# Softmax over tokens on phi as it is loaded, with a maximum from slice comparisons, and filler matmuls tied to other events

## The chip, the cores and the metric

The kernel runs on one core of one Trainium2 chip. The metric is the device time of one execution in microseconds (us), and the median of three runs is quoted. The engines are TensorE (PE in the profile, its weight loads PEld), VectorE (DVE), ScalarE (ACT), GpSimd (POOL) and SyncE (SP), which here only issues transfers.

## The reference, cut to what matters

```python
a = phi - np.max(phi, axis=2, keepdims=True)      # phi [4, 8, 576, 32]: over the 576 tokens
a = np.exp(a)
a = a / (np.sum(a, axis=2, keepdims=True) + 1e-09)
k_m = np.einsum('bhsm,bhsd->bhmd', a, k)          # 32 memory rows for each head
v_m = np.einsum('bhsm,bhsd->bhmd', a, v)
scores = scale * np.matmul(q, k_m.transpose(0, 1, 3, 2))
...                                               # softmax over the 32, times v_m
x = (x @ w_a) * (x @ w_b) @ w_out                 # first gated layer, 2304 x 512, d_ff 1536
...                                               # second one: h * sigmoid(1.702 h), d_ff 2048
```

## The kernel before

**Units.** The attention is worked off in eight units, one for each batch and half of the heads: unit n is batch n // 2, heads 4 (n % 2) to 4 (n % 2) + 3. A tile of phi for a unit holds 128 partitions of tokens (`[P, HG, C0, M]`, 4 heads by 5 chunks of tokens by 32 columns); odd partitions have 4 chunks, and the fifth of theirs is filled once at the start. `memory(n)` takes a unit from phi to the 32 rows of keys and values of each head (`bdk`, `bdv`) and on to the scores; `queries(n)` transposes q for it; `softmax` makes the attention weights and marks them `attn`.

**memory(n) before.** phi is turned so that tokens lie along the free dimension: in units 0 and 1 by 20 matmuls against the identity (L552), in units 2 to 7 by a copy (L540 on GpSimd or L542 on ScalarE) and five transposes (L549). VectorE reduces the maximum over 512 and 64 tokens from PSUM (L556, L558) and joins them (L560). ScalarE takes the exponential with the sum beside it (L562, L566). Five more transposes turn it back (L570, L574), two copies bring it from PSUM into phi's tile (recorded in the helper `copy`, L330 and L332), and 20 matmuls multiply it with keys and values (L590). The result is scaled (L604 or L606), transposed (L612), copied, and multiplied with the queries (L629).

**The first gated layer.** Weights arrive as 64-bit words in pieces (`raw`) and are decoded by two ScalarE instructions and one of VectorE (L438, L442, L444). `fold(g, b)` multiplies the weights of column group g with `bdv` of batch b (L792), `fold_out` splits the product (L810, L812) and `gated` multiplies it with the attention weights (L844). A group needs four decoded pieces, a fold the `bdv` of two units. The rest of the layer and the second one follow (L1006, L1281, L1482, L1513).

**What sets the order.** No engine is scheduled at run time. While the program is built, a planner (`Order`) runs all of these as streams with priorities. It has a clock for each engine and a cost for each step, and emits at each turn the step that it thinks can start first. Loads have modelled landings: `load` adds size / rate to a running DMA time (first value `od.dma`, in ns) and then a latency, both from `RATE0` in this stage. Each engine then executes its instructions in the order that was emitted, and waits for data at run time. The order of the loads is the list `FIRST`: phi, keys and values, and q of units 0 and 1, then raw pieces 0 to 5, then unit 2, and so on.

**Fillers.** The stream `warm_up` has the lowest priority and puts matmuls of the identity with itself into TensorE's order: 18 at once (L1578), then, from the mark `phi 0` (the modelled landing of phi) until the weights of group 0 are decoded, wherever the planner sees TensorE free, each with a planned cost of 300 ns (L1582). Each of these matmuls is two instructions in the profile.

## Time and profile before

| | |
|---|---|
| median of three runs | 744.67 us (744.63 to 747.3) |
| the profiled execution | 744.51 us; span from first to last instruction 742.7 us, so 1.8 us lie around it |
| TensorE | 732.1 us busy (99%), chain that ended last 92% TensorE |
| VectorE, ScalarE, GpSimd | 533.2, 430.8, 386.1 us busy |
| granted TensorE clock | 0.999 in the mean |

Matmuls of fillers count as busy, so TensorE's share of the first 30 us says nothing about useful work. In a row of the profile a number after x is a count of instructions; a bracket at the end of a timeline row is the idle time of that engine ahead of the row and what ended it.

### The profile page before, as it was taken

To read this page: it belongs to the slowest core of one execution; us is meant where nothing else is said; L and a number is where in the kernel's file an instruction comes from. 1 tells how busy PE (TensorE), PEld (TensorE's weight loads), DVE (VectorE), ACT (ScalarE), POOL (GpSimd) and SP (SyncE) were. 2 spreads that over 40 slices of the span, in tenths; PEclk is the share of its full clock that TensorE was granted. 3 is DMA by queue.
4 is the path that set the end of the run, shared out by engine and by line. 5 is a ranking of instruction groups with operands and counts; after the bars stand their busy time and mean duration, and the time that the engine had idled before them with its cause. 6 is when DMAs were issued, how large, how long until landed. Compare 5 with 4: busy or idle time off the path is not lost.

```text
span 742.7 us, 14507 instructions
## 1 busy us (share of the span) xinstructions
PE 732.1 (99%) x5344; PEld 682.7 (92%) x5344; DVE 533.2 (72%) x799; ACT 430.8 (58%) x842; POOL 386.1 (52%) x347
## 2 busy tenths in 40 slices
PE   9899999999999999999999999999999999999997
PEld 8787888888889999999999999999998888999997
DVE  2987777568983447945898666666665697898884
ACT  3678664667863456546866655565656654544441
POOL 0324366447996616914998621333240296776660
PEclk9999999999999999999999999999999999999999
DMA  8998954786778966676525575544699954544411
GB/s 276 343 327 254 322 190 160 224 280 231 256 237 264 313 195 170 171 211 191 186 100 163 180 227 162 163 136 150 210 377 301 328 157 138 189 143 143 143 26 33
DMA packets 110359, 153.53 MB, mean 207 GB/s; under 512 B 8400, under 2 KB 89040, under 8 KB 110288
## 3 DMA queue, kind: packets, MB, share of 16 engines
q1 hardware_dynamic: 104928, 143.13, 60.3%
q10 hardware_dynamic: 5360, 9.47, 3.9%
q8 instruction: 42, 0.69, 0.4%
q14 instruction: 29, 0.24, 0.1%
HBM read 100.01 MB, written 52.56 MB: 205 GB/s over the span
## 4 chain that ended last, share of the span: by engine, by line
PE 92%; DMA 3%; POOL 2%; DVE 2%; SPq 1%; issue 0%; ACT 0%; DVEq 0%; POOLq 0%
PE bank L1281 24%; PE bank L844 21%; PE bank L1006 16%; PE bank L1513 14%; PE bank L1482 12%; PE bank L792 3%; DMA q<-in_q_dram 1%; PE bank L590 1%; DMA raw_p<-in_moe_w_b_dram 1%; DMA kv<-in_k_dram 1%; PE bank L509 1%; POOL w L339 1%; SPq L372 1%; POOL attn L339 1%; DVE attn L339 0%
## 5 line engine op out<-in xcount | busy, mean ns | idle before, releaser
L844 PEld LDWEIGHTS bank<-attn,eff 128*128 128x128 f32 x1152 | 154.3, 188 | 16.2 <-issue 6.1
L844 PE MATMUL bank<-attn,eff 128*128 128x288 f32 x1152 | 163.1, 298 | 0.5 <-DVE eff L812 0.5
L339 POOL TENSOR_TENSOR acc<-acc 128x512 f32<-128x512 f32 (+2 forms) x65 | 95.0, 1481 | 68.2 <-DVE w L339 27.9
L1323 DVE TENSOR_TENSOR acc<-bank,acc 128x384 f32<-128x384 f32 x168 | 89.8, 553 | 46.3 <-PE bank L1281 40.8
L339 DVE TENSOR_TENSOR w<-acc,w 128x512 fp32r<-128x512 f32 (+2 forms) x100 | 105.0, 1076 | 20.5 <-ACT w L345 20.4
L345 ACT ACTIVATE w<-acc 128x512 fp32r<-128x512 f32 (+2 forms) x129 | 74.9, 590 | 65.7 <-PE bank L1513 38.9
L345 ACT ACTIVATE attn<-acc 128x768 fp32r<-128x768 f32 (+2 forms) x80 | 61.0, 769 | 54.5 <-PE bank L1006 38.7
L1006 PE MATMUL bank<-attn,w 128*128 128x384 f32 x504 | 91.8, 335 | 0.8 <-DVE attn L339 0.7
L1006 PEld LDWEIGHTS bank<-attn,w 128*128 128x128 f32 x504 | 87.5, 188 | 2.0 <-DVE attn L339 1.4
L339 DVE TENSOR_TENSOR attn<-acc,attn 128x768 fp32r<-128x768 f32 (+2 forms) x54 | 65.6, 1225 | 31.9 <-ACT attn L345 30.8
L1333 ACT ACTIVATE acc<-acc 128x384 f32<-128x384 f32 x96 | 49.3, 524 | 44.0 <-DVE acc L1323 43.0
L339 POOL TENSOR_TENSOR attn<-acc,attn 128x768 fp32r<-128x768 f32 (+2 forms) x26 | 41.9, 1623 | 35.8 <-ACT attn L345 35.8
L1281 PE MATMUL bank<-attn,w 128*128 128x384 f32 x288 | 55.1, 334 | 0.0
L339 POOL TENSOR_TENSOR w<-dm,w 128x256 fp32r<-128x256 f32 x27 | 24.5, 908 | 57.9 <-ACT w L345 57.9
L888 POOL TENSOR_TENSOR gr<-gr 128x288 f32<-128x288 f32 x48 | 44.6, 931 | 17.0 <-issue 7.0
L339 POOL TENSOR_TENSOR w<-acc,w 128x256 fp32r<-128x256 f32 (+2 forms) x27 | 30.0, 1119 | 44.4 <-ACT w L345 44.3
L1281 PEld LDWEIGHTS bank<-attn,w 128*128 128x128 f32 x288 | 50.4, 188 | 0.0
L1006 PE MATMUL bank<-attn,w1b 128*128 128x384 f32 x252 | 47.6, 336 | 0.2 <-DVE attn L339 0.2
L339 POOL TENSOR_TENSOR sT<-sT,sm 128x576 f32<-128x576 f32 (+1 forms) x12 | 13.5, 1126 | 64.0 <-DVE sm L654 31.7
L1281 PE MATMUL bank<-w1b,w 128*128 128x384 f32 x224 | 46.2, 334 | 0.0
L1006 PEld LDWEIGHTS bank<-attn,w1b 128*128 128x128 f32 x252 | 43.8, 188 | 0.9 <-DVE attn L339 0.5
L1281 PE MATMUL bank<-w 128*128 128x384 f32 x224 | 43.8, 334 | 0.0
(185 smaller groups left out, 1448.9 us busy)
## 6 DMA issues: line engine op xcount, KB each, us to landing
acc<-g1d SPq DMA_DIRECT2D x63, 384.0 KB, 3.8
g2d<-acc SPq DMA_DIRECT2D x96, 192.0 KB, 2.0
raw<-in_moe_w_out_dram SPq DMA_DIRECT2D x24, 512.0 KB, 4.9
acc<-g2d SPq DMA_DIRECT2D x10, 1024.0 KB, 7.6
raw<-in_moe_w_in_dram SPq DMA_DIRECT2D x16, 512.0 KB, 4.3
acc<-g2d SPq DMA_DIRECT2D x16, 512.0 KB, 5.5
g1d<-gr SPq DMA_DIRECT2D x12, 576.0 KB, 4.9
g1d<-acc SPq DMA_DIRECT2D x8, 576.0 KB, 4.8
```

The costliest lines, as they stand in the source:

```text
L339: (nc.gpsimd if e == POOL else nc.vector).tensor_tensor(out=dst, in0=in0, in1=in1, op=op)
L345: nc.scalar.activation(out=hi, in_=src, func=AF.Copy)
L372: nc.sync.dma_start(out=dst.rearrange("p (n f) w -> p n (f w)", n=runs), in_=src)
L792: nc.tensor.matmul(ps[c][0][row(h), :], bdv[b][half, h, :], wt["wab", g, h][0][half, :], start=True, stop=True)
L844: nc.tensor.matmul(dst[:, :U], e[:, c, sw, i * CW + j * P:i * CW + (j + 1) * P], attn(b, mv, c, u * U, U), start=(n == 0), stop=(n == 3 * ...
L888: nc.gpsimd.tensor_tensor(out=dst, in0=in0, in1=in1, op=ALU.subtract)
L1006: nc.tensor.matmul(ps[0][:, :N2], w1_of(a, g, sw)[:, r * P:(r + 1) * P], b[0][:, mv, i], start=(first and q == n == 0), stop=(q == NG1 // ...
L1281: nc.tensor.matmul(ps[0][:, :N2], w[:, sw, r, :], y[mv][r], start=(n == 0), stop=(n == 5))
L1323: nc.vector.tensor_tensor(out=s[0], in0=ps[0][:, :N2], in1=x[0], op=ALU.add)
L1333: nc.scalar.activation(out=c[0], in_=c[0], func=AF.Gelu_apprx_sigmoid)
L1482: nc.tensor.matmul(ps[i, s][0], b[0][:, sw, c - o, :], wo2[c][:, mv], start=(c == n == 0), stop=(c == 4 * K4 - 1 and n == 2),)
L1513: nc.tensor.matmul(ps[name][0][:, :NB], x[0][:, sw, c, :], moving(b, h // 2 + c, mv), start=(h == c == n == 0), stop=(h > 0 and c == K4 - ...
```

## The change

`memory(n)` no longer turns phi. VectorE compares slices of the loaded tile: chunks 0 and 1 with 2 and 3, the two results with each other, and chunk 4 with that, so that each partition has its maximum for 128 columns (head by memory row). One transpose and one `reduce_max` over 128 give the maximum of each column; it is put, negated, on a diagonal (`dg`), and a matmul of a tile of ones with this diagonal spreads it over all partitions (`low`). VectorE adds it to phi (640 elements), ScalarE takes one exponential over 640, and L590's successor reads that. The sum is made by four additions of slices, on VectorE or GpSimd as the planner chooses, and a matmul of one column. All units do the same.

The fillers at the start are 9 instead of 18; the planner then fills TensorE from the moment it expects the first transposed maximum (`turned`) until group 0's weights are decoded, and again from the first fold until the first matmul of `gated` is emitted (`begun`), now at 220 ns each. The first fold is planned 1000 ns (`LATE`) after its data. The modelled loads begin at 2800 ns, with a rate of 335 and a latency of 1700 ns (before 2000, 300 and 2500). `HOLDD`, which kept piece 4's decoding behind the attention weights of unit 1, is gone.

```diff
-HOLDD = {4: ("attn", 1, 0)}
-RATE0 = 300.0, 2500.0
+RATE0 = 335.0, 1700.0
+LEAST = -3.0e38
+LATE = 1000.0
+FILL = 220
-        self.dma, self.marks, self.streams, self.count = 2000.0, {}, [], 0
+        self.dma, self.marks, self.streams, self.count = 2800.0, {}, [], 0
...
-            if i in HOLDD:
-                yield ("mark", *HOLDD[i])
...
     def memory(n):
...
-                nc.tensor.transpose(dst, et[0][:, c].rearrange("p s x -> p (s x)"), ident)
...
-                nc.tensor.matmul(dst[h * M:(h + 1) * M, :], ph[0][:, h, c, :], ident, start=True, stop=True)
...
-        nc.vector.reduce_max(out=m[0], in_=ba[0], axis=AX.X)
...
-            out=et[0][:, :last].rearrange("p c s x -> p (c s x)"), in_=ba[0], func=AF.Exp, bias=m[2], accum_out=m[3]
...
+        top = dg.rearrange("p (h m) -> p h m", h=HG)
+        two, src = et[0][:, :, :2], ph[0]
+        nc.vector.tensor_tensor(out=two, in0=src[:, :, 0:2], in1=src[:, :, 2:4], op=ALU.max)
+        nc.vector.tensor_tensor(out=top, in0=two[:, :, 0], in1=two[:, :, 1], op=ALU.max)
+        nc.vector.tensor_tensor(out=top, in0=top, in1=src[:, :, 4], op=ALU.max)
+        t, bb = yield PE, t, 110, bank_a
+        tp, low, kvp, total = (bb[0][:, i * P:(i + 1) * P] for i in range(4))
+        nc.tensor.transpose(tp, dg, ident)
+        if n == 0:
+            od.mark(t, "turned")
+        nc.vector.reduce_max(out=m[0], in_=tp, axis=AX.X)
+        nc.vector.tensor_scalar(out=dg, in0=ident, scalar1=m[0], scalar2=-1.0, op0=ALU.mult, op1=ALU.mult)
+        nc.tensor.matmul(low, ones, dg, start=True, stop=True)
+        nc.vector.tensor_tensor(
+            out=et[0], in0=ph[0],
+            in1=low.rearrange("p (h u m) -> p h u m", h=HG, u=1).to_broadcast([P, HG, C0, M]), op=ALU.add,
+        )
+        phi_s.release(ph, t)
+        nc.scalar.activation(out=et[0], in_=et[0], func=AF.Exp)
+        t2, e = yield {DVE: 4 * dve(P), POOL: 4 * pool(P)}, t
+        for c in range(1, C0):
+            (nc.gpsimd if e == POOL else nc.vector).tensor_tensor(
+                out=top, in0=et[0][:, :, 0] if c == 1 else top, in1=et[0][:, :, c], op=ALU.add
+            )
...
-                    kvp[h * M:(h + 1) * M, :], ph[0][:, h, c, :], kvs[0][:, :, h, c, :],
+                    kvp[h * M:(h + 1) * M, :], et[0][:, h, c, :], kvs[0][:, :, h, c, :],
...
+        nc.tensor.matmul(total[:, :1], dg, ones[:, :1], start=True, stop=True)
+        nc.vector.tensor_scalar_add(m[1], total[:, :1], 1e-9)
...
     def fold(g, b):
+        if (g, b) == (0, 0):
+            t += LATE
...
     def gated(g, b, u):
+                    od.mark(t, "begun")
...
     def warm_up():
-        _, ps = yield PE, 0.0, 220, bank_m
-        for _ in range(18):
+        _, ps = yield PE, 0.0, 430, bank_m
+        for _ in range(9):
             nc.tensor.matmul(ps[0][:, :P], ident, ident, start=True, stop=True)
-            yield PE, 0.0, 220
-        yield "mark", "phi", 0
-        while ("wab", 0, 2 * NHG - 1) not in od.marks:
+            yield PE, 0.0, 430
+        yield "mark", "turned"
+        yield from fill(ps, bank_m, ("wab", 0, 2 * NHG - 1))
+        yield "mark", "fold", 0, 0
+        _, ps = yield PE, 0.0, 220, bank_a
+        yield from fill(ps, bank_a, ("begun",))
+
+    def fill(ps, owner, until):
+        while until not in od.marks:
             nc.tensor.matmul(ps[0][:, :P], ident, ident, start=True, stop=True)
-            t, _ = yield PE, 0.0, 300
+            t, _ = yield PE, 0.0, FILL
         nc.tensor.matmul(ps[0][:, :P], ident, ident, start=True, stop=True)
-        bank_m.release(ps, t)
+        owner.release(ps, t)
```

In the start-up, the fill value of phi's missing chunk becomes -3.0e38, a tile of ones is set, and the tiles `et` no longer need a fill.

## Rows read from the trace of the kernel before

**Rows 1.** Windows: stretch, length, busy us of each engine, granted clock, DMA share, GB/s.

```profile
0.00:33.33 33.33, 30.06 (x380) 25.70 (x380) 18.34 (x54) 16.24 (x38) 5.17 (x12) 1.00 0.92 307
33.33:62.25 28.92, 26.70 (x310) 21.69 (x308) 25.73 (x57) 23.25 (x54) 8.40 (x10) 1.00 0.96 313
62.25:700.00 637.75, 636.76 (x4340) 596.96 (x4341) 459.69 (x653) 377.24 (x729) 353.88 (x316) 1.00 0.65 208
```

**Rows 2.** Timeline of TensorE, start and length in us, to the first gated matmul.

```profile
6.96 1.50 PE L1582 MATMUL bank<-ident 128*128 128x128 f32 x12
8.40 1.30 PE L552 MATMUL bank<-ident,phi 128*32 128x128 f32 x40
...
19.50 1.30 PE L590 MATMUL bank<-kv,phi 128*32 128x128 f32 x40
...
30.05 1.07 PE L792 MATMUL bank<-acc,gr 64*32 64x512 f32 x10 [0.23 <-DVE acc L444]
32.81 0.76 PE L549 MATMUL bank<-ident,et 128*128 128x128 f32 x5 [1.69 <-POOL et L540]
33.33 0.90 PE L844 MATMUL bank<-attn,eff 128*128 128x288 f32 x5
```

**Rows 3.** Tile phi, issues of SP up to 3 us (unit 0), issue to landing.

```profile
L355 SPq DMA_DIRECT2D phi<-in_phi_dram x1: 618/618/618, 1.8 to 1.8; - x1
...
DMA to landing us min/median/max: 2.8/3.1/3.3
```

**Rows 4.** Tile kv, issues between 8.5 and 10.2 us (values of unit 1).

```profile
L355 SPq DMA_DIRECT2D kv<-in_v_dram x1: 614/614/614, 9.5 to 9.5; - x1
...
DMA to landing us min/median/max: 6.0/6.0/6.0
```

**Rows 5.** Tile raw_p, issues from 15.8 to 17.5 us (pieces 2 and 3).

```profile
L372 SPq DMA_DIRECT2D raw_p<-in_moe_w_b_dram x2: 430/432/434, 16.3 to 17.3; - x2
...
DMA to landing us min/median/max: 5.7/6.0/6.3
```

**Rows 6.** Chain that ended last: start, length in us, what.

```profile
37.17 0.44 PE bank L570 x4
```

**Rows 7.** Groups by line and shape, 0 to 130 us: busy us, mean ns, idle before.

```profile
L339 POOL TENSOR_TENSOR sT<-sT,sm 128x288 f32<-128x288 f32 x5 | 4.4, 890 | 27.9 <-DVE mx L599 19.8 <-DVE sm L654 7.7 <-DVE sm L663 0.4
...
L812 DVE TENSOR_TENSOR eff<-bank,eff 128x512 fp32r<-128x512 f32 x20 | 12.7, 678 | 1.5 <-ACT eff L810 1.5
...
L868 DVE TENSOR_TENSOR gr<-bank,gr 128x288 f32<-128x288 f32 x19 | 8.7, 456 | 6.9 <-PE bank L844 6.3 <-ACT raw_p L442 0.3
...
L562 ACT ACTIVATE et<-bank,mx 128x512 f32<-128x512 f32 x8 | 5.5, 685 | 11.8 <-DVE mx L560 11.5 <-ACT acc L438 0.3
...
L556 DVE TENSOR_REDUCE mx<-bank 128x1 f32<-128x512 f32 x8 | 5.4, 678 | 7.8 <-PE bank L552 7.8
...
L332 DVE COPY qT<-bank 128x512 f32<-128x512 f32 x6 | 4.0, 685 | 0.8 <-PE bank L509 0.7
...
L558 DVE TENSOR_REDUCE mx<-bank 128x1 f32<-128x64 f32 x8 | 1.6, 204 | 0.0
...
L542 ACT ACTIVATE et<-phi 128x640 f32<-128x640 f32 x2 | 1.5, 740 | 0.0
```

**Rows 8.** Timeline of VectorE, two operations of one shape.

```profile
23.96 0.46 DVE L339 TENSOR_TENSOR sT<-sT,sm 128x288 f32<-128x288 f32 x1
...
27.12 0.93 DVE L339 TENSOR_TENSOR attn<-aT,attn 128x288 fp32r<-128x288 f32 x1
```

**Rows 9.** Timeline of GpSimd, 20 to 28 us.

```profile
21.11 0.67 POOL L339 TENSOR_TENSOR sT<-sT,sm 128x288 f32<-128x288 f32 x1 [19.81 <-DVE mx L599]
26.69 1.05 POOL L339 TENSOR_TENSOR sT<-sT,sm 128x288 f32<-128x288 f32 x1 [4.90 <-DVE sm L654]
```

**Rows 10.** Line L1578 on TensorE, 1.3 to 4 us: ns min, median, max.

```profile
L1578 PE MATMUL bank<-ident x12: 421/421/582, 1.4 to 3.9; 128*128 128x128 f32 x12
```

**Rows 11.** The same line, 5 to 7 us.

```profile
L1578 PE MATMUL bank<-ident x20: 275/275/275, 4.7 to 6.9; 128*128 128x128 f32 x20
```

More of the change, by code (lines that the diff above doesn't have):

```diff
@@ L23 @@
 W1 = 0.0
-HOLD = {}
 PR = 30
@@ L543, in memory @@
-        part = 240 if n < NHG else 70
-        t, ba = yield PE, t, part * last, bank_a
-        t1, bb = yield PE, t, part, bank_a
-        for c in range(C0):
-            dst = (ba if c < last else bb)[0][:, c % last * P:(c % last + 1) * P]
-            if n >= NHG:
-                nc.tensor.transpose(dst, et[0][:, c].rearrange("p s x -> p (s x)"), ident)
-                continue
-            for h in range(HG):
-                nc.tensor.matmul(dst[h * M:(h + 1) * M, :], ph[0][:, h, c, :], ident, start=True, stop=True)
@@ L553, in memory @@
-        even = bb[0][:, :P].rearrange("p (s x) -> p s x", x=2)[:, :, 0]
-        t, mx = yield DVE, t, dve(512), mx_s
-        m = [mx[0][:, i:i + 1] for i in range(6)]
-        nc.vector.reduce_max(out=m[0], in_=ba[0], axis=AX.X)
-        t, _ = yield DVE, max(t, t1), dve(64)
-        nc.vector.reduce_max(out=m[1], in_=even, axis=AX.X)
-        t, _ = yield DVE, t, 70
-        nc.vector.tensor_scalar(out=m[2], in0=m[0], scalar1=m[1], scalar2=-1.0, op0=ALU.max, op1=ALU.mult)
-        t, _ = yield ACT, max(t, et[1]), act(512, True) + 190
@@ L562, in memory @@
-        nc.scalar.activation(
-            out=et[0][:, :last].rearrange("p c s x -> p (c s x)"), in_=ba[0], func=AF.Exp, bias=m[2], accum_out=m[3]
-        )
-        t2, _ = yield ACT, t, act(64, True) + 190
-        nc.scalar.activation(out=et[0][:, last, :, 0], in_=even, func=AF.Exp, bias=m[2], accum_out=m[4])
-        t, _ = yield PE, t, 70 * last
-        for c in range(last):
-            nc.tensor.transpose(
-                ba[0][:, c * P:(c + 1) * P], et[0][:, c].rearrange("p s x -> p (s x)"), ident
-            )
@@ L573, in memory @@
-        t1, _ = yield PE, t2, 70
-        nc.tensor.transpose(bb[0][:, P:2 * P], et[0][:, last].rearrange("p s x -> p (s x)"), ident)
-        et_s.release(et, t1)
-        t1 = yield from copy(
-            t1, ph[0][:, :, last, :], bb[0][:, P:2 * P].rearrange("p (h m) -> p h m", h=HG), P
-        )
-        t = yield from copy(
-            t, ph[0][:, :, :last, :].rearrange("p h c m -> p c h m"),
-            ba[0].rearrange("p (c h m) -> p c h m", c=last, h=HG), 512,
-        )
-        bank_a.release(ba, t)
@@ new lines, in memory @@
+        tp, low, kvp, total = (bb[0][:, i * P:(i + 1) * P] for i in range(4))
+        nc.tensor.transpose(tp, dg, ident)
+        if n == 0:
+            od.mark(t, "turned")
+        t, mx = yield DVE, t, dve(P), mx_s
+        m = [mx[0][:, i:i + 1] for i in range(2)]
+        nc.vector.reduce_max(out=m[0], in_=tp, axis=AX.X)
+        t, _ = yield DVE, t, dve(P)
+        nc.vector.tensor_scalar(out=dg, in0=ident, scalar1=m[0], scalar2=-1.0, op0=ALU.mult, op1=ALU.mult)
+        t, _ = yield PE, t, 220
@@ L1617, in tile_mem_attention_moe_moe2 @@
         last = C0 - 1
-        unused = [s[0][:, :, last, :] for s in phi_s.free] + [s[0][:, last] for s in et_s.free]
-        unused += [s[0][:, i, :, last, :] for s in kv_s.free for i in range(2)]
-        for t in [zero, *unused]:
+        for s in phi_s.free:
+            nc.vector.memset(s[0][:, :, last, :], LEAST)
+        nc.vector.memset(ones, 1.0)
+        for t in [zero] + [s[0][:, i, :, last, :] for s in kv_s.free for i in range(2)]:
             nc.vector.memset(t, 0.0)
```

36 lines of the change are left out of this document (16 added, 20 removed).

## The prediction

> **What bounds the kernel now.** I read the page first: TensorE is busy 99% of the span and makes up 92% of the chain that ended last. Busy includes the fillers, so I cut the span by stages next [rows 1]. From 62.25 to 700 us TensorE is idle for 637.75 - 636.76 = 1.0 us: whatever work is taken from it there comes off the end, if the others keep up. From 33.33 to 62.25 us it is idle for 28.92 - 26.70 = 2.2 us, and VectorE is busy 25.73 of the 28.92 us (0.89), so there the two set the pace together. Before 33.33 us TensorE has hardly any work that counts: the first gated matmul (L844) starts there [rows 2], and what lies ahead of it is the fillers, units 0 and 1 and the first fold. So three numbers matter: when L844 starts, how much work TensorE has after that, and how much it idles up to 62 us.
>
> What holds L844 back? The timeline of TensorE and the landings answer it. phi of unit 0 has landed at 1.84 + 3.3 = 5.1 us [rows 3], but its first matmul runs at 8.40, right behind a row of fillers without a gap [rows 2]. The last values of unit 1 are there at 9.5 + 6.0 = 15.5 us [rows 4], and their matmuls start at 19.50, 4.0 us later. The fourth weight piece has landed at 17.3 + 6.3 = 23.6 us [rows 5]; the first fold waits for its decoding until 30.05. Decoding one piece is two ScalarE passes over 512 elements and one of VectorE, about 2 x 0.69 + 0.68 = 2.1 us if I take L562's and L812's length for them [rows 7], so 25.7 us is possible, 4.3 us earlier. The emitted order runs behind the data by about 4 us, and the transfers are not what it waits for.
>
> **The change part by part.** The profiled execution took 744.51 us (span 742.7 and 1.8 around it), 0.16 below the median, so the sum is made against 744.5.
>
> Start of L844. Phi's first use moves from TensorE, where fillers stand ahead of it, to VectorE, which has no fillers. The load model also moves: up to the fourth piece FIRST brings 6.23 MB, which the old numbers land at 2.0 + 20.8 + 2.5 = 25.3 us and the new ones at 2.8 + 18.6 + 1.7 = 23.1 us, against 23.6 measured [rows 5]. The chain of unit 0 after landing is three comparisons, transpose, reduction, diagonal, matmul, addition and exponential: some 1.0 + 0.3 + 0.6 + 0.3 + 0.8 + 0.7 us and hops, so that the exponential ends near 10 to 11 us and its product waits for keys and values, not for phi. Both delays seen above (4.0 and 4.3 us) can go; 1.0 us is given back by LATE. I take 3.0 us earlier. The bounds are 4.3 us earlier and 1.0 us later (the delays stay and LATE is added). The fillers behind the first fold cost nothing while they end before the first gated matmul's data; at most one planned length, 0.2 us, is lost there, inside these bounds.
>
> TensorE's work. Units 2 to 7 each lose ten transposes, 0.11 us each [rows 6], 1.10 us. They gain one transpose (0.11), a 128-column matmul of two instructions (0.21 to 0.23, as a filler pair: twelve in 1.3 to 1.5 us [rows 2]) and a matmul of one column, for which no row exists: between 0 and the 0.22 of the full one, I take 0.14, nearer the upper end because its weights are 128 columns wide all the same. That is 0.47, net -0.63 per unit, -3.8 us over six units; the bounds are -3.0 and -4.6. Units 0 and 1 count nothing, since fillers surround them.
>
> VectorE. A unit loses L556 (0.68), L558 and L560 (about 0.20 each) = 1.08 us. It gains, by the line through L868 (0.456 at 288) and L812 (0.678 at 512) [rows 7]: 0.43 for 256 elements, two of 0.30, a reduction of 0.27 over 128 (between L558 and L556), 0.30 for the diagonal and 0.81 for 640, together 2.41; net +1.3. Against that go the copies back into phi that fell to VectorE, and the planner can move L332's copies of q (six of 0.685, 0.5 per unit) to ScalarE, which loses two exponentials, the copies and the copy of phi, and gains one pass of 0.74 (as L542). I take +0.4 per unit on VectorE if the four additions go to GpSimd. GpSimd is busy 8.40 of 28.92 us [rows 1], and four additions cost it between 4 x 0.40 (0.890 scaled from 288 to 128) and 4 x 0.89 us; they run beside the 1.2 us of the product, and up to 2 us of the upper bound would show only in the scaling behind it, which TensorE's gated matmuls cover from 33 us on. On VectorE they cost 4 x 0.30 less the overlap of neighbours, about 1.0 us.
>
> Idle time up to 62 us. It can fall by the 2.2 us that are there, since loads are no longer planned late, or grow by the 1.8 us of TensorE work that leaves this stretch (25 of the 60 transposes less the additions of three units) if VectorE sets the pace. I take +0.6, above the middle, since VectorE is at 0.89 and gets no less work.
>
> The missing HOLDD lets decoding of pieces 4 and 5 slip ahead of unit 1's softmax; a VectorE step of 0.68 us is the price, inside the bounds of the start. The other start-up fills are a few tenths ahead of any data.
>
> Sum: -3.0 - 3.8 + 0.6 = -6.2, so 744.5 - 6.2 = 738.3 us. With all terms at their ends: -4.3 - 4.6 - 2.2 = -11.1 (733.4) and +1.0 - 3.0 + 1.8 = -0.2 (744.3).
>
> One row speaks against the change. A VectorE operation on two SBUF tiles of 288 elements took 0.46 us while GpSimd was idle and 0.93 us while GpSimd ran a two-input operation [rows 8, 9]. The change brings three such operations to VectorE and four to GpSimd per unit. The Trainium skill (GPSIMD Engine Reference, Specifications) says that GpSimd shares its SBUF interfaces with VectorE and that VectorE instructions with two SBUF inputs contend for them; the rows agree, by the factor of two just given. By that rule, if it always struck, the time would be that of the second rival below.
>
> **The rivals.** First, the head start is lost to the next wait: L844 begins earlier, but the second group's weights, units 2 and 3, or VectorE come no sooner, and the 2.2 us of idle time grow by as much. For it: 0.89 on VectorE. Against it: those data were planned late too. What is left is TensorE's own work and the idle time: -3.8 + 0.6 = -3.2, so 741.3 us.
>
> Second, slower: VectorE becomes the bound between 33 and 62 us. The four additions go to VectorE (+1.0) and contention doubles both them (+1.0) and the comparisons (+1.0), with +1.3 less the 0.4 that other copies give back, so 3.9 us per unit. Three units take their maximum in this stretch; if VectorE can't be used above the 0.89 seen, that is 3 x 3.9 / 0.89 = 13.1 us, against 3.0 for the early start and 2.0 for the work that TensorE loses after 62 us: +8.1, 752.6 us. It decides from 1.5 us per unit (no gain left: 3 x 1.5 / 0.89 = 5.0); 2.6 us make it slower by 3.7. Against it: GpSimd is idle for 70% of the stretch, so the planner has a free place for the additions.
>
> Third, the low clock. With 9 fillers instead of 18, TensorE goes idle until phi has been compared and transposed. In the opening the same instruction took 421 ns at first and 275 later [rows 10, 11], the lower of the two levels (1.2 and 2.4 GHz) and the upper. After the 1.69 us gap at 31 us the granted clock stayed at 1.00 [rows 1, 2]; the gap here would be about as long (fillers end near 5, the transpose comes after 6). If the level falls, fillers planned at 220 ns take twice that for some 3 us, as long as in the opening, and push what stands behind them by 1.5 us: 739.8 us. The Trainium skill (TensorE: Matmul & The Clock Gate, What's actually happening) puts it that throttled is the default and activity lifts it; no run here yet shows which way this gap goes.
>
> **How the numbers follow.** About 3.7 us (0.5%) can be told from no change here. My forecast has a chance of 0.57, the low clock beside it 0.10, a larger gain still (the idle time gone too, under 733.4) 0.05, the lost head start 0.17, the slower case 0.11. The lost head start (741.3) falls in the band of no change, and of the forecast's range the top three microseconds do too, perhaps 0.03 of chance; the slower case counts as slower by three quarters. So faster 0.69, same 0.22, slower 0.09. The forecast's own bounds are 733.4 to 744.3; a part of the slower case and the larger gain push it to 732 to 746, which leaves out about 0.13.
>
> **What would show it.** L844 should start near 30 us, phi's first VectorE instruction near 5.2, unit 1's product near 16; after 62 us each unit should take 0.6 us less of TensorE, and the stretch from L844's start to 62 us should idle 2 to 3 us. The additions should stand on GpSimd. The forecast is wrong if L844 starts after 32 us, if VectorE's share between L844's start and 62 us passes 0.95 with TensorE waiting for it, or if the emitted order opens gaps after 80 us, where none are now; the last I cannot work out from rows, since one new order replaces another, and it is part of the width.

## The result: 751.4 us, slower by 0.7% where 738.3 was forecast

The changed kernel took 751.38 us (median of 4 runs, 751.06 to 752.55), the kernel before 745.89 (744.63 to 747.3, 4 runs with those shown ahead). The ratio is 1.0068, with a 95% interval of 1.005 to 1.0086. That is slower by more than the 0.5% that the prediction took for what can be told, if only just at the interval's lower end, and outside the range of 732 to 746. The median of the kernel before mixes two kinds of execution: of the 62 beside the later kernels, 27 took 744.4 to 746.0 us at a mean granted clock of 0.999 or 1.000, like its profiled one, and 35 took 746.5 to 747.9 us at 0.996 to 0.998. The profiled execution took 751.06 us, its span is 749.3 (before: 744.51 and 742.7).

Three points cut the 6.55 us between the spans: the first gated matmul (L829, before L844), the first matmul of the layer's second half (L991, before L1006), and that half's end. Each time below is read from the trace of one profiled execution.

| us | before | after | difference |
|---|---|---|---|
| start of the first gated matmul | 33.33 | 37.40 | +4.07 |
| from there to the second half | 208.76 | 208.57 | -0.19 |
| second half of the first layer | 133.86 | 136.52 | +2.67 |
| the rest (all of the second layer) | 366.8 | 366.8 | 0.0 |

The windows of the changed kernel, in the stretches and columns of [rows 1]:

```profile
0.00:33.33 33.33, 30.22 (x308) 26.67 (x308) 20.12 (x59) 15.63 (x31) 8.14 (x17) 1.00 0.89 290
33.33:62.25 28.92, 27.83 (x322) 22.97 (x322) 26.43 (x64) 19.75 (x44) 8.04 (x10) 1.00 0.97 315
62.25:700.00 637.75, 630.66 (x4271) 589.14 (x4270) 464.59 (x658) 372.23 (x708) 352.54 (x321) 1.00 0.64 207
```

From 62.25 to 700 us TensorE now idles 637.75 - 630.66 = 7.1 us, where it was 1.0. VectorE is busy 26.43 of 28.92 us in the second stretch, 0.91 against 0.89: hardly more than before in this stretch (over the whole span it is 546.8 us against 533.2). From the later start on, 37.40 to 62.25 us, TensorE does not idle at all, so its gaps lie behind 62 us.

The timeline of TensorE in the changed kernel, up to the first gated matmul, against [rows 2]:

```profile
6.87 0.47 PE L541 MATMUL bank<-ident,mc 128*128 128x128 f32 x1 [1.30 <-DVE mc L538]
...
18.42 1.30 PE L569 MATMUL bank<-kv,et 128*32 128x128 f32 x40
...
23.50 0.72 PE L611 MATMUL bank<-qT,bdk 64*32 64x288 f32 x16
24.15 6.07 PE L1573 MATMUL bank<-ident 128*128 128x128 f32 x52
30.06 0.39 PE L1575 MATMUL bank<-ident 128*128 128x128 f32 x2
30.37 1.64 PE L776 MATMUL bank<-acc,gr 64*32 64x512 f32 x16
31.95 0.94 PE L1573 MATMUL bank<-ident 128*128 128x128 f32 x6
34.42 0.33 PE L541 MATMUL bank<-ident,mc 128*128 128x128 f32 x1 [1.54 <-DVE mc L538]
34.59 2.62 PE L1573 MATMUL bank<-ident 128*128 128x128 f32 x22
37.04 0.60 PE L510 MATMUL bank<-ident,q 128*128 128x128 f32 x4
37.40 0.77 PE L829 MATMUL bank<-attn,eff 128*128 128x288 f32 x4
```

Three things stand here. Fillers run without a gap from 24.15 us into the fold (L776), which ends at 32.01 us; before it ended at 30.05 + 1.07 = 31.12, so +0.89. The last fillers (L1573 at 34.59) and transposes of q stand ahead of L829. And between them lies the split of the fold's product, on ScalarE (L794) and VectorE (L796).

The fillers right ahead of the fold do not set its end. Its second part, 10 of the 16 matmuls, needs the fourth weight piece, whose decoding ends on VectorE. VectorE's row of that piece in the changed kernel, then in the kernel before:

```profile
30.22 0.67 DVE L445 SCALAR_TENSOR_TENSOR acc<-acc,raw_p 128x512 uint32<-128x512 uint32 x1
```

```profile
29.30 0.69 DVE L444 SCALAR_TENSOR_TENSOR acc<-acc,raw_p 128x512 uint32<-128x512 uint32 x1
```

They end at 30.89 and 29.99 us, and the second part begins at 30.95 and 30.05; in all twenty kernels it begins 0.05 or 0.06 us behind that end. So the +0.89 is VectorE's. Unit 1's scores (L611, before L629), whose softmax stands ahead of the later pieces on VectorE, are done a little earlier than before, at 23.50 + 0.72 = 24.22 us against 23.91 + 0.71 = 24.62:

```profile
23.91 0.71 PE L629 MATMUL bank<-qT,bdk 64*32 64x288 f32 x16
```

The split in the changed kernel:

```profile
32.32 0.66 ACT L439 ACTIVATE acc<-raw_p 128x512 f32<-128x512 f32 x1
32.88 0.66 ACT L443 ACTIVATE raw_p<-raw_p 128x512 uint32<-128x512 uint8 x1
33.43 1.07 ACT L794 ACTIVATE eff<-bank 128x512 fp32r<-128x512 f32 x2
```

```profile
32.46 0.42 DVE L536 TENSOR_TENSOR et<-phi 128x256 f32<-128x256 f32 x1
32.92 0.64 DVE L537 TENSOR_TENSOR mc<-et 128x128 f32<-128x128 f32 x1
33.60 0.77 DVE L538 TENSOR_TENSOR mc<-mc,phi 128x128 f32<-128x128 f32 x1
...
34.77 0.62 DVE L445 SCALAR_TENSOR_TENSOR acc<-acc,raw_p 128x512 uint32<-128x512 uint32 x1
35.32 1.27 DVE L796 TENSOR_TENSOR eff<-bank,eff 128x512 fp32r<-128x512 f32 x2
```

These are timelines of ScalarE and VectorE of the changed kernel. The product is complete at 32.01, but ScalarE decodes a later weight piece first (L439, L443) and begins the split at 33.43. VectorE has unit 2's comparisons and another decoding step ahead of its part, which ends at 36.59. From the fold's end to the split's end that is 4.58 us. Before it was 2.13, with the split's end at 33.25:

```profile
31.13 1.08 ACT L810 ACTIVATE eff<-bank 128x512 fp32r<-128x512 f32 x2 [2.28 <-PE bank L792]
```

```profile
32.00 1.25 DVE L812 TENSOR_TENSOR eff<-bank,eff 128x512 fp32r<-128x512 f32 x2
```

From the split's end to L829 it is 0.81 us, before 0.08. So the start's +4.07 is 0.89 from the fold, 2.45 from what ScalarE and VectorE have ahead of the split, 0.73 from the last fillers and the transposes of q.

The second half of the first layer shows its +2.67 in TensorE's waits (us in total, times, longest), the changed kernel from 246 to 383 us, then the kernel before from 242 to 376:

```profile
PE bank L991 <- POOL attn L342: 2.5, 3, 1.1
PE bank L991 <- DVE attn L342: 1.3, 2, 0.8
```

```profile
PE bank L1006 <- DVE attn L339: 0.9, 3, 0.5
```

### The profile page after: what moved, and what is told of

It reads as the page before. It is cut to its first block, busy times and chain, and to the rows that moved or that the text cites. A ratio compares the mean times of both kernels' runs of the same rounds, so it can differ in the third digit from the quotient of the medians.

```text
span 749.3 us, 14342 instructions
## 1 busy us (share of the span) xinstructions
PE 733.8 (98%) x5272; PEld 683.7 (91%) x5272; DVE 546.8 (73%) x825; ACT 424.6 (57%) x809; POOL 393.3 (52%) x361
## 4 chain that ended last, share of the span: by engine, by line
PE 84%; POOL 5%; DVE 4%; DMA 3%; issue 2%; SPq 1%; ACT 1%; DVEq 0%; ACTq 0%; POOLq 0%
PE bank L1266 23%; PE bank L829 16%; PE bank L991 15%; PE bank L1498 13%; PE bank L1467 12%; PE bank L776 2%; POOL attn L342 1%; DVE attn L342 1%; POOL grp L873 1%; DMA raw_p<-in_moe_w_b_dram 1%; DMA raw<-in_moe_w_b_dram 1%; DMA phi<-in_phi_dram 1%; POOL mc L561 1%; POOL w L342 1%; PE bank L510 0%
## 5 line engine op out<-in xcount | busy, mean ns | idle before, releaser
L829 PEld LDWEIGHTS bank<-attn,eff 128*128 128x128 f32 x1152 | 154.3, 188 | 16.9 <-issue 5.5
L829 PE MATMUL bank<-attn,eff 128*128 128x288 f32 x1152 | 163.1, 298 | 0.9 <-DVE eff L796 0.8
L342 POOL TENSOR_TENSOR acc<-acc 128x512 f32<-128x512 f32 (+2 forms) x63 | 91.3, 1472 | 69.0 <-DVE w L342 27.6
L342 DVE TENSOR_TENSOR w<-acc,w 128x512 fp32r<-128x512 f32 (+2 forms) x101 | 103.3, 1048 | 19.0 <-ACT w L348 19.0
L991 PE MATMUL bank<-attn,w 128*128 128x384 f32 x504 | 91.4, 335 | 1.7 <-POOL attn L342 1.1
L991 PEld LDWEIGHTS bank<-attn,w 128*128 128x128 f32 x504 | 87.6, 188 | 2.4 <-POOL attn L342 1.4
L991 PE MATMUL bank<-attn,w1b 128*128 128x384 f32 x252 | 48.0, 336 | 2.1 <-POOL attn L342 1.3
L991 PEld LDWEIGHTS bank<-attn,w1b 128*128 128x128 f32 x252 | 43.9, 188 | 3.1 <-POOL attn L342 2.0
L1266 PEld LDWEIGHTS bank<-w1b,w 128*128 128x128 f32 x224 | 39.5, 188 | 0.0
```

Of the source, the lines that this page charges most:

```text
L342: (nc.gpsimd if e == POOL else nc.vector).tensor_tensor(out=dst, in0=in0, in1=in1, op=op)
L829: nc.tensor.matmul(dst[:, :U], e[:, c, sw, i * CW + j * P:i * CW + (j + 1) * P], attn(b, mv, c, u * U, U), start=(n == 0), stop=(n == 3 * ...
L991: nc.tensor.matmul(ps[0][:, :N2], w1_of(a, g, sw)[:, r * P:(r + 1) * P], b[0][:, mv, i], start=(first and q == n == 0), stop=(q == NG1 // ...
L1266: nc.tensor.matmul(ps[0][:, :N2], w[:, sw, r, :], y[mv][r], start=(n == 0), stop=(n == 5))
```

## Experiments

Eighteen kernels ran. Each entry gives the median in us and its ratio to the kernel before with the 95% interval. Then "start" is that of the first gated matmul, "stretch" the time from there to the second half, "half" the second half of the first layer, and "low" how long after the start the granted clock was 0.5. For the changed kernel these are 37.40, 208.6, 136.5 and 0, for the kernel before 33.33, 208.8, 133.9 and 0. All four are read from one profiled execution, which need not take the median time (after_land_1900: 749.56 against 747.25). The time at which the granted clock reached 1.00 is the first record of it in the trace. The windows count the time ahead of that record as 1.00, but fillers there have the lower level's length: 422 ns until 9.5 us and 276 from 10.9 in the changed kernel, as in [rows 10, 11].

### Which part of the change costs: each half alone

**memory_alone**: the new `memory`, everything else as before (this diff, like those of all entries but rest_alone and the three whose names begin with before, is to the changed kernel).

```diff
+HOLDD = {4: ("attn", 1, 0)}
...
-RATE0 = 335.0, 1700.0
+RATE0 = 300.0, 2500.0
...
-LATE = 1000.0
+LATE = 0.0
...
-        self.dma, self.marks, self.streams, self.count = 2800.0, {}, [], 0
+        self.dma, self.marks, self.streams, self.count = 2000.0, {}, [], 0
...
+            if i in HOLDD:
+                yield ("mark", *HOLDD[i])
...
     def warm_up():
...
+        for _ in range(18):
...
+        yield "mark", "phi", 0
...
+            t, _ = yield PE, 0.0, 300
...
```

> The new memory(n), with everything else as before: old fillers, old load model, HOLDD, no LATE. Three theories of why the first gated matmul starts at 37.4 us in the changed kernel and at 33.3 before. A, fillers and clock: the shorter opening lets the clock of TensorE stay at the lower level to 10.5 us (4.5 before), and fillers at 220 ns leave no room to catch up; then this run starts gating at 32 to 34 us. B, order: without HOLDD the decoding of pieces 4 and 5 stands ahead of unit 1's softmax; then this one starts at 33 to 34.5 us as well. C, VectorE: the comparisons and the wide addition themselves are too much; then this one starts at 36 us or later. The stretch of the first layer's second half (first to last matmul of project) was 133.9 us before and 136.5 after; if the new memory as such costs that, it is 136 to 137 here, and if it is an accident of the emitted order it can be anything from 133.5 to 137.

757.79, 1.0159 (1.0139 to 1.018); start 33.30, stretch 219.5, half 136.5, low 6.0. The start is that of A and B and not of C; the half fits either reading of it.

**rest_alone**: the old `memory` with the new fillers, load model and LATE, without HOLDD (the diff is to the kernel before).

```diff
-HOLDD = {4: ("attn", 1, 0)}
...
-RATE0 = 300.0, 2500.0
+RATE0 = 335.0, 1700.0
...
+LATE = 1000.0
+FILL = 220
...
+        yield "mark", "turned"
+        yield from fill(ps, bank_m, ("wab", 0, 2 * NHG - 1))
+        yield "mark", "fold", 0, 0
+        _, ps = yield PE, 0.0, 220, bank_a
+        yield from fill(ps, bank_a, ("begun",))
```

> The old memory(n) with the new fillers, load model, LATE and no HOLDD. A: gating starts 1.5 us later than before or more, at 35 to 37 us, since the opening and the fillers are those of the changed kernel. B: 35 to 37 us too. C: 31 to 34 us, as before or better. Time by A or B 746 to 750 us, by C 740 to 745.

753.16, 1.0095 (1.0071 to 1.012); start 35.69, stretch 215.1, half 134.1, low 0. Again the start is that of A and B, but the time lies above all that was expected.

Each half alone is slower than both halves together. The costs don't add, so neither can be read as a fixed cost of that half's work. The late start comes with the rest: with the new `memory` alone it stays at 33.30, and with the new load model alone (before_new_loads, below) at 33.47, which leaves the new fillers, LATE and the missing HOLDD, or these together with the load model.

### The late start

**hold_back**: the changed kernel with the decoding of piece 4 held behind unit 1's attention weights again.

```diff
+HOLDD = {4: ("attn", 1, 0)}
...
+            if i in HOLDD:
+                yield ("mark", *HOLDD[i])
```

> The changed kernel with HOLDD again, so that piece 4 and what follows is decoded only once the attention weights of unit 1 are planned. B: gating starts at 33 to 35 us, time 747 to 749. A and C: 36.5 to 37.5 us, time within 1 us of the changed kernel's 751.

755.48, 1.0129 (1.0106 to 1.0153); start 38.44, stretch 215.4, half 133.9, low 3.4. The start came later still: the granted clock reached 1.00 only at 13.3 us (10.5 in the changed kernel) and the fold began at 32.09. From the fold's modelled end (32.09 + 1.64 = 33.73 us) to the start it was still 4.7 us. Neither expectation was met: bringing HOLDD back does not bring the start back, and the time is 4 us above the changed kernel's.

**long_opening**: 22 opening fillers at 220 ns instead of 9 at 430.

```diff
-        for _ in range(9):
+        for _ in range(22):
...
-            yield PE, 0.0, 430
+            yield PE, 0.0, 220
```

> The changed kernel with 22 opening fillers at 220 ns, so that TensorE has work until the first transpose of unit 0. All theories: granted clock at the upper level from about 4.5 us instead of 10.5. A: unit 1's transpose and the products of units 0 and 1 come 1 to 2 us earlier, and gating starts at 35 to 36 us, time 749 to 750. B and C: gating still starts at 36.5 to 37.5 us, since VectorE and ScalarE hold it.

751.26, 1.0074 (1.0053 to 1.0096); start 37.87, stretch 209.2, half 136.5, low 0. The clock reached 1.00 at 7.1 us, 3.4 us earlier, and nothing was gained: the longer row of fillers runs to the first transpose of unit 0, which begins at 9.11 us instead of 6.87, and the fold began at 30.85 us. The start lies above what either expectation named.

**fill_300**: the fillers' planned length alone.

```diff
-FILL = 220
+FILL = 300
```

> The changed kernel with fillers planned at 300 ns, as before the change, instead of 220, so that TensorE can make up for time lost to the low clock. A, fillers: the product of unit 1 and the first fold come 1.5 to 2 us earlier (fold at 28.5 to 29, 30.4 now), gating starts at 35 to 36 us, time 749 to 750. B, order on ScalarE and VectorE: gating starts within 0.7 us of 37.4.

748.31, 1.0033 (1.002 to 1.0046); start 33.40, stretch 212.1, half 134.2, low 3.4. The timeline of TensorE:

```profile
26.36 1.42 PE L776 MATMUL bank<-acc,gr 64*32 64x512 f32 x6
28.76 1.07 PE L776 MATMUL bank<-acc,gr 64*32 64x512 f32 x10 [0.98 <-DVE acc L445]
...
33.40 0.77 PE L829 MATMUL bank<-attn,eff 128*128 128x288 f32 x4
```

The fold begins 4.0 us earlier, at 26.36, but TensorE then idles 0.98 us for decoded weights, and it ends 2.2 us earlier, at 29.83. Unit 1's scores are done 2.2 us earlier too (21.28 + 0.72 = 22.00 us), and so is the decoding of the fourth piece (28.71). So the fillers delay the fold by way of unit 1's scores and VectorE. Fold and start come earlier than A named, and far from B. In the changed kernel's timeline the fillers' 52 instructions, 26 pairs, run from 24.15 to 30.06 us, 0.23 us for each. Planned at 220 ns they leave TensorE no time to make up for a delay, while at 300 ns each leaves 70. The clock reached 1.00 at 4.5 us in this run, but that is not the reason: in fill_300_no_late, below, it was 9.7 us, with the scores done at 21.87.

**unit2_waits**: the changed kernel in which unit 2's `memory` and the decoding from piece 4 on wait until the first fold has been split, in the plan.

```diff
+            if i == 4:
+                yield "mark", "eff", 0, 0, 1
...
+        if n == 2:
+            yield "mark", "eff", 0, 0, 1
```

> The changed kernel; unit 2's memory(n) and the decoding from piece 4 on are planned only behind the split of the first fold's product. A: the fold stays at 30.4 and gating starts at 36.5 to 37.4 us. B: between the fold and the first gated matmul nothing but unit 1's softmax and the split is left, so gating starts at 34.5 to 35.5 us; what follows may idle more, since unit 2 comes later, so that the time is 749 to 752.

754.42, 1.0121 (1.0087 to 1.0156); start 34.10, stretch 219.1, half 133.9, low 13.7. The timelines of TensorE and ScalarE:

```profile
29.83 1.64 PE L780 MATMUL bank<-acc,gr 64*32 64x512 f32 x16
31.40 2.94 PE L1577 MATMUL bank<-ident 128*128 128x128 f32 x24
34.10 1.09 PE L833 MATMUL bank<-attn,eff 128*128 128x288 f32 x5
```

```profile
31.77 1.07 ACT L798 ACTIVATE eff<-bank 128x512 fp32r<-128x512 f32 x2
```

The fold is nearly as late as in the changed kernel, and ends at 29.83 + 1.64 = 31.47 us. But ScalarE splits its product at once, from 31.77, and the start is 3.3 us earlier. So the fillers' planned length and the order on ScalarE and VectorE both matter, and changing either brings the start back to about 34. The start is 0.4 us earlier than B named, the time 2.4 us above its range.

**no_second_fill**: no fillers behind the first fold.

```diff
-        yield "mark", "fold", 0, 0
-        _, ps = yield PE, 0.0, 220, bank_a
-        yield from fill(ps, bank_a, ("begun",))
```

> The changed kernel without the fillers behind the first fold (those from the fold to the first gated matmul). A: gating starts 0.4 to 0.8 us earlier, at 36.6 to 37, since 11 fillers stand between the transposed maximum of unit 2 and the queries ahead of it; the granted clock may fall in the gap. B: the start is within 0.3 us of 37.4.

758.0, 1.0161 (1.0139 to 1.0183); start 35.74, stretch 214.3, half 140.1, low 16.3. The start is 1.7 us earlier, more than A named, and behind the fold the clock falls to 0.5 in three stretches, from 34.9, 65.7 and 267 us.

### The second half of the layer, and the order as such

**nudge**: the planner's clock of TensorE is put 1.2 us on when the last gated matmul has been emitted. No work changes, and the order up to there is the same.

```diff
         room_gated()
+        od.clock[PE] += 1200.0
         crowded()
```

> The changed kernel; only the planner's clock of TensorE is set 1200 ns forward where the first layer's second half (project) is planned, which changes which engine gets which of the low parts there, and no work. If the 2.7 us that this half takes longer than before (136.5 against 133.9) is an accident of the emitted order, it takes 133.5 to 134.5 here and the whole 748 to 749.5. If it comes from the new softmax or from the later start, it stays at 136.3 to 136.8 and the whole at 751.

748.13, 1.0032 (1.0016 to 1.0047); start 36.95, stretch 208.4, half 133.9, low 0. TensorE's waits in the second half, in the columns of the changed kernel's rows above:

```profile
PE bank L991 <- DVE attn L342: 0.9, 3, 0.5
```

The 2.6 us are gone, as the first reading had it, with the same work; TensorE's own order is the same from end to end, and only ScalarE, VectorE and GpSimd have theirs changed, in the second half. Ahead of it the start is 0.45 us earlier, where the order of all engines is the same and the clock is not, which reached 1.00 at 6.2 instead of 10.5 us in this run: so about so much of the late start can be put down to the low clock.

If a shift of a clock in the plan is worth 2.6 us, the kernel before must be asked the same. Three kernels with the old work change only the planner's numbers for loads; nothing else of the change is in them.

```diff
-RATE0 = 300.0, 2500.0
+RATE0 = 300.0, 2300.0
```

> The kernel before with one number of the load model changed: the planned latency of a load in the first stage is 2300 instead of 2500 ns. No work changes, only the order in which the planner emits it. Theory A (an early order of this kernel is worth several us, and the order of the kernel before happens to be a good one; any other number gives a worse draw): 747 to 754 us, with the stretch from the first gated matmul to the second half of the layer at 211 us or more instead of 208.8. Theory B (the changed kernel is slower because of its new operations, and orders differ by little): within 0.3% of the kernel before.

757.65, 1.0156 (1.0133 to 1.0178); start 33.57, stretch 222.6, half 133.9, low 6.8. Windows of this kernel (columns as in [rows 1]):

```profile
33.57:62.25 28.68, 26.83 (x274) 23.33 (x282) 22.37 (x49) 21.91 (x51) 7.79 (x10) 0.88 0.93 299
62.25:256.18 193.93, 188.67 (x1716) 159.16 (x1701) 136.28 (x219) 117.25 (x233) 116.98 (x112) 1.00 0.70 229
```

TensorE idles 193.93 - 188.67 = 5.3 us in the second of them, and the granted clock of the first is 0.88: the same work of the kernel before, in another order, takes 13.9 us longer from the start to the second half.

**before_new_loads** has the new load model whole, as in the diff ahead (start 2800, rate 335, latency 1700):

> The kernel before with the new load model alone (start 2800, rate 335, latency 1700), nothing else of the change. Theory A (an order drawn anew costs some us, whatever the reason for which it was drawn): 747 to 754 us. Theory B (only the fillers and the new operations cost): within 0.3% of the kernel before, with the first gated matmul at 32 to 34 us.

755.6, 1.0131 (1.0105 to 1.0157); start 33.47, stretch 213.2, half 139.7, low 0.

**before_land_2700** has a latency of 2700:

> The kernel before with a planned load latency of 2700 instead of 2500 ns; only the order changes. Theory A (the order of the kernel before is a rare good one): 749 us or more, as with 2300 ns (757.7). Theory B (2300 ns was a bad draw, and the old order is a usual one): 743 to 748 us.

754.49, 1.0112 (1.008 to 1.0143); start 33.60, stretch 216.4, half 136.8, low 6.8. Its waits in the second half:

```profile
PE bank L1006 <- POOL attn L339: 2.4, 4, 1.1
PE bank L1006 <- DVE attn L339: 1.3, 2, 0.8
```

These are the waits of the changed kernel, in a kernel with none of the change. All three draws are 1.1 to 1.6% slower than the kernel before, and 3 to 6 us slower than the changed kernel. Theory A holds, and more strongly than it was put: two of the three lie above the range it gave.

### Other orders of the changed work

Each of these changes planner numbers of the changed kernel alone. fill_260 has fillers at 260 ns; fill_300_no_late has them at 300 and LATE at 0; after_land_1900 a planned load latency of 1900.

> The changed kernel with fillers planned at 260 ns. Theory A (the fillers planned at 220 ns hand the slow start on to the first fold, and slack in their plan takes the delay up): the first fold between 26.4 and 30.4 us, so the first gated matmul between 33.4 and 37.4 us; in all 745 to 752 us, since the order behind it is drawn anew. Rival (it is ScalarE's and VectorE's order alone that delays the start): the start stays at 37 us or later even where the fold comes earlier.

> The changed kernel with fillers planned at 300 ns and without the 1000 ns by which the first fold is planned later. If the fold's planned delay counts at run time too, the first gated matmul starts up to 1.0 us before the 33.4 us of the kernel with 300 ns alone; if the fold waits for data, as in the kernel before, it stays at 33.4. In all 744 to 751 us: with the stretch behind the start at 208.5 us and the second half of the layer at 133.9 us the span would be 742.6 us, and 4 us more with a stretch as in the kernel with 300 ns alone.

> The changed kernel with a planned load latency of 1900 instead of 1700 ns; only the order changes. Theory A (its time is set by the order that happens to be drawn, with a scatter of several us): anywhere from 746 to 757 us, and at least 2 us away from 751.4. Theory B (the loss belongs to the changed work): 751.4 within 1.5 us, with the first gated matmul at 37 us or later again.

The next four start from fill_300_no_late: a latency of 1900 (f3_land_1900), of 1800 (f3_land_1800), piece 4 held back again (f3_hold), and fillers at 320 (fill_320_no_late).

> The changed kernel with fillers planned at 300 ns, no LATE, and a planned load latency of 1900 ns. Theory A (slack in the fillers sets the start, the rest is the draw): the first gated matmul between 32 and 34 us, and the time anywhere from 743 to 753 us. Theory B (745.7 us of the kernel without the shift is what this work takes once the fillers have slack): 745.7 within 1.5 us.

> The changed kernel with fillers planned at 320 instead of 300 ns and no LATE. Theory A (slack sets the start, the rest is the draw): the first gated matmul between 32 and 34 us, the time anywhere from 743 to 753 us. Theory B (slack alone sets the time): 745.7 within 1.5 us.

> The changed kernel with fillers planned at 300 ns, no LATE, and a planned load latency of 1800 ns. If the early start comes with the slack, the first gated matmul lies between 31.5 and 34.5 us as in the three kernels of this kind; the time between 742 and 754 us, below 744 only if the stretch behind the start is 209 us or less and the second half of the layer 134.

> The changed kernel with fillers planned at 300 ns, no LATE, and the decoding of piece 4 held behind unit 1's attention weights as in the kernel before. If holding it back keeps ScalarE and VectorE free for the split of the first fold, the first gated matmul lies at 32.5 us or earlier; since the order is drawn anew, 742 to 757 us in all.

| | median | ratio (95%) | start | stretch | half | low |
|---|---|---|---|---|---|---|
| fill_260 | 755.33 | 1.013 (1.0099 to 1.0162) | 36.17 | 214.5 | 135.7 | 3.4 |
| fill_300_no_late | 745.67 | 0.999 (0.9978 to 1.0002) | 32.46 | 210.2 | 133.9 | 0 |
| after_land_1900 | 747.25 | 1.0019 (1.0004 to 1.0034) | 36.62 | 208.8 | 135.5 | 0 |
| f3_land_1900 | 745.39 | 0.9989 (0.9976 to 1.0001) | 34.38 | 209.5 | 133.9 | 0 |
| fill_320_no_late | 754.02 | 1.0113 (1.0082 to 1.0145) | 31.54 | 216.9 | 136.6 | 10.2 |
| f3_land_1800 | 750.38 | 1.0066 (1.0041 to 1.0092) | 33.53 | 211.8 | 136.5 | 3.4 |
| f3_hold | 749.85 | 1.0054 (1.0032 to 1.0077) | 32.90 | 212.0 | 136.5 | 3.4 |

Against fill_300, fill_300_no_late starts 33.40 - 32.46 = 0.94 us earlier without LATE; the fold itself comes only 0.12 us earlier, but ScalarE has one decoding pass less ahead of the split, which begins at 29.72 instead of 30.22. Where fillers have slack, a slow clock does not reach the start: in fill_300_no_late the clock rose at 9.7 us, nearly as late as in the changed kernel, and the fold began at 26.24 all the same. With a rise at 13.2 us (f3_land_1900, whose plan is 0.2 us later too) the fold began at 28.17. The six kernels with fillers at 300 ns or more, and unit2_waits, start between 31.5 and 34.4 us; the seven others of the changed work with the new fillers at 220 or 260 start at 35.7 to 38.4. Yet the earliest start belongs to one of the slowest kernels (fill_320_no_late, with 7.1 us idle in the stretch). Where an expectation named a number for the start, f3_land_1900 (34.38, over 34), fill_320_no_late (31.54, under 32) and f3_hold (32.90, over 32.5) missed it. Of the times, those of fill_260 (over 752) and fill_320_no_late (over 753) lie above the ranges named. The two lowest times are level with the kernel before; their intervals include 1.

## Why the prediction was wrong

**Start of L844: predicted -3.0, bounds -4.3 and +1.0, measured +4.07.** This is the step that failed. It took the 4.0 and 4.3 us between landing and use [rows 2, 4, 5] for delays that would go once phi's first use no longer stood behind fillers. The first part was right: VectorE took phi at 5.74 us, as it landed, against 5.2 forecast. But unit 1's product ran at 18.42 us, not near 16, and its scores were done only 0.4 us earlier than before, since the same fillers stood ahead of everything behind that first use, now without slack. And the other delay did not go at all. The prediction had the fourth piece decoded 2.1 us behind its landing, at 25.7 us, as if ScalarE and VectorE were free for it. VectorE was done with it at 30.89 us, 0.90 later than before, because the first three pieces and the softmax of unit 1 stand ahead of it there. The earliest of the twenty kernels (fill_320_no_late) had it at 27.33; with the fillers at 300 and no LATE the fold begins at 26.24, but it waits for that piece until 28.64, and the first gated matmul, at 32.46, gained only 0.9 us. Further, "at most one planned length, 0.2 us" for the fillers behind the fold was 0.73 with the transposes of q. The price given to the missing HOLDD and to what VectorE and ScalarE hold ahead of the split, "0.68 us, inside the bounds", was 2.45 us; hold_back shows that HOLDD is not the reason by itself.

**TensorE's work: predicted -3.8, measured -2.1.** The mechanism is right and the size is off, outside the bounds too (-3.0 and -4.6; from the prediction's own terms they come to -3.2 and -4.7). Counted from each matmul's start to the next one's, between the start and the second half 55 transposes at 5.69 us went, not 60 at 6.6, because unit 2's first five stood ahead of the start [rows 2]. What came (L541, L550, L576) took 3.60 us instead of 2.82; the column matmul alone is 0.24 for its pair, where 0.14 was taken, the upper bound being 0.22.

**Idle time: predicted +0.6 up to 62 us, measured -2.2 there and +3.3 behind it.** TensorE idled 2.2 us between the start and 62.25 us before and not at all after; from 62.25 us to the second half it idled not at all before and 3.3 us after, 1.2 of them for the additions on GpSimd (L561), which the prediction held to be covered by gated matmuls. Together that is +1.1. (Its upper bound, 1.8, comes to 1.3 with the 0.47 that it used for the additions of a unit.) Queries, gated matmuls and one filler took 0.9 us more together, so of the -2.1 only 0.19 us was left.

**The second half of the layer: not in the sum, +2.67.** The prediction named gaps after 80 us as something that it could not work out from rows; they came. nudge shows that they belong to one order, and before_land_2700 that the old work has them too.

**Rivals.** The first, the head start lost to the next wait, had no head start to lose. The second one, VectorE as the bound between 33 and 62 us, did not happen: 0.91 with 1.1 us of TensorE idle in the second stretch. But ahead of the start VectorE did set the pace, busy from 24.31 us to the split's end with one gap of 0.20 us, and its contention is seen there. L537 and L538 took 0.64 and 0.77 us at 33 us (VectorE's rows above); at 6 us, with GpSimd idle, they took 0.29 each. Rows of VectorE at 6 us and of GpSimd at 33:

```profile
6.20 0.29 DVE L537 TENSOR_TENSOR mc<-et 128x128 f32<-128x128 f32 x1
6.52 0.29 DVE L538 TENSOR_TENSOR mc<-mc,phi 128x128 f32<-128x128 f32 x1
```

```profile
32.61 0.81 POOL L342 TENSOR_TENSOR sT<-sT,sm 128x288 f32<-128x288 f32 x1 [1.19 <-DVE sm L643]
33.38 0.84 POOL L342 TENSOR_TENSOR attn<-aT,attn 128x288 fp32r<-128x288 f32 x1
```

The decoding shows the same. The two steps of it (L445) that begin right behind the start of a GpSimd operation take 1.13 and 1.29 us, the one of 30.22 us above, begun with GpSimd idle, 0.67:

```profile
25.48 1.13 DVE L445 SCALAR_TENSOR_TENSOR acc<-acc,raw 128x512 uint32<-128x512 uint32 x1
...
27.62 1.29 DVE L445 SCALAR_TENSOR_TENSOR acc<-acc,raw_p 128x512 uint32<-128x512 uint32 x1
```

```profile
25.40 1.75 POOL L342 TENSOR_TENSOR sT<-sT,sm 128x288 f32<-128x288 f32 x2 [4.81 <-ACT raw L443]
27.56 0.81 POOL L342 TENSOR_TENSOR attn<-aT,attn 128x288 fp32r<-128x288 f32 x1 [0.41 <-ACT attn L348]
```

The four pieces take 3.85 us of VectorE in the changed kernel, 2.76 before and 2.70 in fill_320_no_late, where the fold ends earliest (28.46 us). No run here changes this contention alone, so its share of the late start is not shown.

The Trainium skill (GPSIMD Engine Reference, Specifications) says that VectorE and GpSimd share SBUF interfaces, with contention where a VectorE instruction has two SBUF inputs, and the trace agrees, by a factor of 2.2 to 2.7 for L537 and L538. The additions stood on GpSimd in four units (1, 4, 5 and 6, counted in order of time) and on VectorE in the others, not on GpSimd throughout as forecast. The third rival, the low clock, happened: the granted clock stayed at the lower level until 10.5 us, after a gap of 1.30 us, where it rose at 4.5 before; nudge puts its price at about 0.45 us, where the rival had 1.5; in hold_back a rise 2.8 us later goes with a start 1.0 us later. The slower case came by a way that no rival had: the emitted order, ahead of the start and again in the second half, of work that takes TensorE itself no longer.

**What the loss belongs to.** Of the order alone it is shown that 200 ns in a planned latency move the kernel before by 1.1 to 1.6%. The changed work with its new fillers took from 745.4 to 758.0 us in fourteen orders, the old work 753.2 to 757.7 in four orders other than the one before. So the change replaced an order that was good for its work, which none of the four others was, by one that was fair. That the changed work would be faster in an order equally good is what the -2.1 suggests, but it is not shown: the best one found is level.

**What stays open.** Why one order takes 208.8 and another 222.6 us from the start to the second half, with the same work. In before_land_2300 TensorE idles 4.9 us more there than in the kernel before (7.1 against 2.2) and is busy 9.0 us longer (215.5 against 206.5); the 6.8 us at half the clock can make up 3.4 of that. Of the twenty kernels, the eleven in which the granted clock was at 0.5 for a time behind the start all took 211.8 us or more; of the nine others seven took 208.4 to 210.2. So the low clock goes with the long stretches, but two are long without it (213.2 and 215.1), and what makes it fall is not settled: a gap of 1.69 us left it at 1.00 [rows 2].

## What to carry to other kernels

Where a planner writes the order, a change of work draws a new order, and its scatter (here some 12 us) can be larger than what the work is worth (2 us): move an irrelevant number of the plan in both kernels before judging the change. A filler planned at its exact length leaves no room to catch up, and an early delay goes on to the first real work; plan it longer, and ask which steps of other engines the planner can put between the first product and its consumer. That an engine is busy up to a step does not mean that it holds the step: the fold began right behind fillers, but its end followed VectorE's decoding in every kernel. Work that leaves the bounding engine is a gain only if the steps that it waits for don't move: sum the start, the stretch and the gaps separately.

## What was not expected of the hardware

A matmul of one column took TensorE as long here as one of 128 columns with weights of the same shape. The line of L576 in the changed kernel (ns min, median, max) and its neighbours in TensorE's timeline:

```profile
L576 PEld LDWEIGHTS bank<-ones,mc x16: 186/188/190, 14.4 to 108.9; 128*128 128x128 f32 x16
L576 PE MATMUL bank<-ones,mc x16: 250/261/272, 14.4 to 109.0; 128*128 128x1 f32 x16
```

```profile
44.44 0.38 PE L576 MATMUL bank<-ones,mc 128*128 128x1 f32 x2
44.69 1.84 PE L829 MATMUL bank<-attn,eff 128*128 128x288 f32 x12
46.37 0.38 PE L550 MATMUL bank<-mc,ones 128*128 128x128 f32 x2
46.59 0.39 PE L1575 MATMUL bank<-ident 128*128 128x128 f32 x2
```

The pair with one column holds TensorE for 44.69 - 44.44 = 0.25 us, that with 128 columns for 46.59 - 46.37 = 0.22; the median of the weight load is 188 ns for both (L576 and L550).

The time at which the granted clock first reached 1.00 differed between executions whose order to that point is the same: 10.5 us in the changed kernel, 6.2 in nudge. After the start it was at 0.5 for 3.4 to 16.3 us in eleven kernels, with no row that tells why. In the 3.4 us of fill_300 (52.3 to 55.7 us) the gated matmul's median is 442 ns, ahead of them 295. L829 there from 52.4 to 55.6 and from 40 to 49 us (ns min, median, max):

```profile
L829 PE MATMUL bank<-attn,eff x12: 382/442/589, 52.2 to 55.3; 128*128 128x288 f32 x12
```

```profile
L829 PE MATMUL bank<-attn,eff x26: 290/295/400, 39.7 to 44.4; 128*128 128x288 f32 x26
```
